# Loads, order and products of the first batch, and the place of the first chunk's forms, in a fused attention and mixture kernel

## The chip, the core and the metric

The kernel runs on one core of a Trainium2 chip. The metric is the device time of one execution in microseconds (us). Before the change, five runs gave 1661.59 to 1662.9 us, median 1661.75.

The core's engines are called by their short names in the profile: PE is TensorE (matrix products), PEld its weight loads, DVE is VectorE, ACT is ScalarE, POOL is GpSimd, SP is SyncE, which here only issues transfers (DMAs).

## The reference

All data is float32. First an attention without softmax: for each of 8 batches and 8 heads, with 576 tokens and 64 columns,

```python
kv = np.einsum('bhsd,bhse->bhde', k, v)
out = np.einsum('bhsd,bhde->bhse', q, kv)
rms = np.sqrt(np.mean(out * out, axis=-1, keepdims=True) + 1e-06)
x = out / rms * g_norm          # then (batch, token, head * column): 4608 x 512
```

Then a mixture of four experts, w1 of 512 x 1024 and w2 of 1024 x 512 each:

```python
p = domain_probs / (domain_probs.sum(-1, keepdims=True) + 1e-09)
for e in range(4):
    h = np.maximum(x @ w1[e], 0.0)
    out += p[:, e:e + 1] * (h @ w2[e])
```

## The kernel before, in words

**Chunks and steps.** The 4608 tokens are nine chunks of 512. Chunk c below 8 holds 512 tokens of batch c; chunk 8 holds the 64 tokens that are left of each batch. A step s is one chunk with one expert: s = 9 e + c, 36 steps. `up` makes h of a step, `down` or `down_deep` the second product and the sum into the output, one step later.

**Products.** A product of blocks is done by a scheme with seven products instead of eight, nested twice in most steps. It needs sums and differences ("forms") of blocks of x, w1, w2 and h, which VectorE or GpSimd computes (`combine`, line 433). `x_forms` (line 1124) makes those of a chunk's x in expert 0: four of 512 columns, seven of 256 and fourteen of 128 (25 sums), and stores them with x itself in DRAM by nine DMAs; `x_again` (line 1178) loads them for the experts 1 to 3 into five buffers `xf`. Chunk 0 in expert 0 is the exception: `up_plain` (line 1320) multiplies it in the plain way, 64 products with 512 columns (two records of the trace each), so that work can begin before any form is there. The forms of chunk 0 are made after that and serve the later experts only. Nearly all products are issued by `halves_of` (line 406): two halves of 64 output rows each; their line in the profile is 410.

**The opening** (line 688) is the attention of batch 0, by pairs of heads hp = 0 to 3. For each pair:
- `load_pair` (line 702) issues three DMAs: q with four tokens to a partition (token 4p + r, 512 tokens, 128 partitions, two pieces of 1024 bytes in each), k and v with six tokens to a partition (96 partitions, two pieces of 1536 bytes).
- `turn` (line 748) transposes q: eight products with the identity, 128 rows, 64 output rows, 128 columns (line 753).
- `key_values` (line 767): twelve products of 96 rows and 64 columns (line 772). ScalarE copies both results out of PSUM (lines 762, 785).
- `attend` (line 792): sixteen products of 64 rows and 64 columns (line 799) that use all four quarters of the array, the two row halves into two different banks `raw`.
- `scaled` (line 646): ScalarE squares (661), VectorE sums (668), ScalarE takes a root (628), VectorE inverts and scales (635 to 640, 678).
- `turn_x` (line 814): four transposes (line 817); ScalarE copies x with the gain to `xh` (line 825).

The 64 tokens that are left of batch 0 have their own load of q, four transposes (line 843) and eight products (line 861). `up_plain` needs a whole half of x (two pairs) for each of its products' operands.

**What sets the order.** Every operation is handed to a planner (`Plan`) with a key, a cost for each engine that can do it, and what it reads and writes. `layout` (line 91) plays the costs through and writes one fixed order per engine. PE takes the first operation by key that is ready, the others the one that is due first. CROSS (line 52) is the time that it counts between engines, `bus` the state of the transfers, SPARE, REACH and due times keep buffers back. Sums between SBUF buffers carry `port=True`: the planner lets VectorE and GpSimd do them one at a time, and a GpSimd sum waits for the VectorE sum planned before it (line 1734). When PE has nothing ready early on, the planner puts in fills (`idle`, line 1713: two transposes of the identity; line 1715). SP issues DMAs in planned order on eight semaphore lanes.

**Transfers in the opening.** SP issues the q, k, v of four pairs, with the gains after the second pair, then the four quarters of w1 (512 KB each, pieces of 2048 bytes), then q, k, v of batch 1, w2, and from 38.00 us the probabilities (`norm_probs`, line 446: seven DMAs, mostly pieces of 16 bytes). `result` (line 1366) writes the output rows; chunk 0's rows follow q's order of tokens, 4p + r.

Of the kernel before, what the change touches and what calls it, by code (L numbers as in the profile page):

```python
# [11 lines left out]
ALU = mybir.AluOpType  # L12
# [27 lines left out]
class Plan:  # L40
# [11 lines left out]
    CROSS, SAME, LANES = 0.3, 0.06, 8  # L52
# [38 lines left out]
    def layout(self, slots, later, idle, idle_banks, idle_until):  # L91
# [58 lines left out]
        bus, port = 3.8, 0.0  # L150
# [33 lines left out]
        while left:  # L184
# [4 lines left out]
            for eng in todo:  # L189
# [32 lines left out]
                if best is not None:  # L222
                    op = best
                    op.start, op.eng = t, eng
                    if eng == "SP":
                        busy[eng] = t + op.cost[eng]
                        bus = max(bus, t + 1.5) + op.kb / 215.0
                        op.end = bus + 0.5
                        lanes = lanes[1:] + [op.end]
                    else:  # L230
                        op.end = busy[eng] = t + op.cost[eng]
                        if op.kb:
                            op.end += 9.0 if op.kb == 512 else 8.0
# [62 lines left out]
def kernel(  # L296
# [76 lines left out]
    for kind, n in BANKS.items():  # L373
# [15 lines left out]
    slots["w2y"] = [w2y_home[:, i, :] for i in range(2)]  # L389
    later = [  # L390
        (("kv", "kvbd"), "w2y", [kv_home[:, i, :] for i in range(3)]),
# [37 lines left out]
    def combine(key, cost, out_, a, b, op, reads, writes):  # L429

        plan.add(
            key, cost,
            lambda eng: adder(eng).tensor_tensor(out=out_(), in0=a(), in1=b(), op=op),  # L433
            reads=reads, writes=writes, port=True,
        )
# [10 lines left out]
    def norm_probs(key):  # L446
        by_batch = moe_domain_probs.rearrange("(b s) e -> s b e", s=S)

        def load_all(eng):
            nc.sync.dma_start(  # L450
                out=p_all[:, 0:NR, :],
                in_=moe_domain_probs[0:NT, :].rearrange("(p r) e -> p r e", r=NR),
            )
            for r in range(NR):
                nc.sync.dma_start(
                    out=p_all[:, NR + r:B * NR:NR, :], in_=by_batch[r * P:(r + 1) * P, 1:, :])
            for bb in range(2):
                nc.sync.dma_start(
                    out=p_all[bb * REM:(bb + 1) * REM, B * NR:NBLK, :],
                    in_=by_batch[NT:S, bb::2, :],  # L460
                )
# [10 lines left out]
        plan.add(key, {"SP": 4.0}, load_all, writes=[probs], kb=72)  # L472
# [34 lines left out]
    def weights_1(e, key, step, need):  # L507
# [4 lines left out]
        for i, (n, dh, uh) in enumerate(((1, 0, 0), (2, 1, 0), (21, 0, 1), (4, 1, 1))):  # L512
# [3 lines left out]
                key + i * step, f[n],  # L516
                lambda n=n: f[n].ap[:].rearrange("p (k u) -> p k u", k=2),
                w1_src(e, dh, uh), 512 if e else 312, also=[corner[n]],
            )

        def form(k_, o, a, b, op):
# [3 lines left out]
                [f[a], f[b], corner[a], corner[b]], [f[o], corner[o]],  # L525
# [41 lines left out]
    def weights_2(e, key, step, deep):  # L567

        f = {n: Buf("big", f"w2_{e}_{n}") for n in (1, 12, 2, 3, 5, 6, 7, 4)}
        for i, (n, uh, dh) in enumerate(((1, 0, 0), (2, 1, 0), (12, 0, 1), (3, 1, 1))):  # L570
# [3 lines left out]
                w2_src(e, uh, dh), 512,  # L574
# [71 lines left out]
    def scaled(key, name, raw, n, x, blocks):  # L646
# [8 lines left out]
        def src(r):  # L655
            return raw[r].ap[0:n, 0:width].rearrange("p (b d) -> p b d", d=D)

        for r in range(2):
# [3 lines left out]
                    out=x.ap[0:n, r * width:(r + 1) * width], in_=raw[r].ap[0:n, 0:width],  # L662
                    func=ACT.Square),
                reads=[raw[r]], parts=[x],
# [10 lines left out]
        for r in range(2):  # L675
            plan.add(
# [8 lines left out]
                reads=[raw[r], rt], **{"parts" if r else "writes": [x]},  # L685
            )

    def opening(key, span, rem):
# [8 lines left out]
        at = lambda j: key + span * j / (NPAIR + 1)  # L697
        qTs, kvs = {}, {}

        splits = ((96, 6, 0),)  # L700

        def load_pair(hp):
            hs = slice(2 * hp, 2 * hp + 2)
            n = f"{b}_{hp}"
            kt, vt, qt = Buf("big", f"k{n}"), Buf("big", f"v{n}"), Buf("big", f"q{n}")
            want = key - 1 + 0.1 * hp
            load(
                want, qt, lambda qt=qt: qt.ap[:, 0:NT].rearrange("p (h x) -> p h x", h=2),
                q[b, hs, 0:NT, :].rearrange("h (p r) d -> p h (r d)", r=NR), 172,
            )  # L710
            for t, src in ((kt, k), (vt, v)):
                at_ = 0
                for rows, n_, size in splits:
                    load(
                        want, t,
                        lambda t=t, at_=at_, rows=rows, n_=n_: t.ap[0:rows, at_:at_ + 2 * n_ * D]
                        .rearrange("p (h x) -> p h x", h=2),
                        src[b, hs, size:size + rows * n_].rearrange("h (p j) d -> p h (j d)", j=n_),
                        241,
                    )  # L720
                    at_ += 2 * n_ * D
            return kt, vt, qt

        def kv_rows(t):

            at_ = 0
            for rows, n_, _ in splits:
                for j in range(n_):
                    yield [
                        t.ap[0:rows, at_ + (h * n_ + j) * D:at_ + (h * n_ + j + 1) * D]  # L730
                        for h in range(2)
                    ]
                at_ += 2 * n_ * D

        groups = ((0,), (1,), (2,), (3,))
        for g, pairs in enumerate(groups):
            n = f"{b}_{g}"
            kbank = Buf("ab", f"kv{n}")
            kv = Buf("kvbd", f"kvc{n}")
            held = []  # L740
            for o, hp in enumerate(pairs):
                kvs[hp] = kv, o
                kt, vt, qt = load_pair(hp)
                held.append((kt, vt))
                bank = Buf("ab", f"qT{b}_{hp}")
                qT = qTs[hp] = Buf("big", f"qT{b}_{hp}")

                def turn(eng, bank=bank, qt=qt):
                    for r in range(NR):
                        rs = slice(r * P, (r + 1) * P)  # L750
                        for o in range(2):
                            at = (o * NR + r) * D
                            nc.tensor.matmul(  # L753
                                bank.ap[o * D:(o + 1) * D, rs], lhsT=qt.ap[:, at:at + D],
                                rhs=ident[:],
                            )

                plan.add(
                    at(hp), {"PE": 0.82}, turn, reads=[qt], writes=[bank])
                plan.add(  # L760
                    at(hp), act(NT),
                    lambda eng, bank=bank, qT=qT: nc.scalar.activation(
                        out=qT.ap[:, 0:NT], in_=bank.ap[:], func=ACT.Copy),
                    reads=[bank], writes=[qT],
                )

            def key_values(eng, bank=kbank, held=held):
                for o, (kt, vt) in enumerate(held):
                    sets = list(zip(kv_rows(kt), kv_rows(vt)))
                    for j, (ks, vs) in enumerate(sets):  # L770
                        for r in range(2):
                            nc.tensor.matmul(  # L772
                                bank.ap[r * D:(r + 1) * D, o * D:(o + 1) * D],
                                lhsT=ks[r], rhs=vs[r], start=(j == 0),
                                stop=(j == len(sets) - 1), skip_group_check=True,
                            )

            size = len(pairs)
            plan.add(
                at(pairs[-1]), {"PE": 0.73 * size + 0.2}, key_values,  # L780
                reads=[t for ts in held for t in ts], writes=[kbank],
            )
            plan.add(
                at(pairs[-1]), act(size * D),
                lambda eng, bank=kbank, to=kv, size=size: nc.scalar.activation(
                    out=to.ap[:, 0:size * D], in_=bank.ap[:, 0:size * D], func=ACT.Copy),
                reads=[kbank], writes=[kv],
            )
            kind = ("db", "u2", "u1", "db")[g]
            raw = [Buf(kind, f"raw{n}_{r}") for r in range(2)]  # L790

            def attend(eng, raw=raw, kv=kv, pairs=pairs):
                for o, hp in enumerate(pairs):
                    for i in range(NR):
                        for c in range(2):
                            for r in range(2):
                                half = slice(r * D, (r + 1) * D)
                                at = i * P + c * D
                                nc.tensor.matmul(  # L799
                                    raw[r].ap[c * D:(c + 1) * D, (o * NR + i) * D:(o * NR + i + 1) * D],  # L800
                                    lhsT=qTs[hp].ap[half, at:at + D],
                                    rhs=kv.ap[half, o * D:(o + 1) * D],
                                )

            plan.add(
                at(pairs[-1] + 0.4), {"PE": 0.5 * size + 0.2}, attend,
                reads=[qTs[hp] for hp in pairs] + [kv], writes=raw,
            )
            x = Buf("big", f"xg{n}")
            scaled(at(pairs[-1] + 0.4), n, raw, P, x, size * NR)  # L810
            for o, hp in enumerate(pairs):
# [954 lines left out]
```

## Time and profile before

| what | value |
|---|---|
| median of five runs | 1661.75 us (1661.59 to 1662.9) |
| the profiled execution's own time | 1661.64 us |
| its span, first to last instruction | 1659.5 us |
| granted PE clock, mean | 0.999 |
| PE busy in the stretches 62 to 185, 463 to 830, 830 to 1200 us | 122.95 of 123, 366.95 of 367, 370.00 of 370 |
| PE busy from 0 to 22 us, fills among it | 19.80 of 22 |
| DMA, 2 to 16 us | 247 GB/s, share 0.99 of 16 engines |
| issue of q, k, v of pair 0 and time to landing | 0.75 + 2.9, 1.25 + 3.4, 1.75 + 4.7 us |
| issue of k, v of pair 3 and time to landing | 9.20 + 7.4, 10.53 + 7.3 us |

How to read it: "busy" of PE is the time in which at least one product is under way; fills are among it. A line of a time line has start, length, engine, line of the kernel, operation, out <- in, shape and number of records, and in brackets how long the engine had been idle and what ended that. A line of the table of stretches has the stretch, its length, busy time and number of records of PE, PEld, DVE, ACT and POOL (an engine without records is left out of the heading when only some are asked for), the granted PE clock, the busy share of the 16 DMA engines and GB/s. A line of waits has engine and line, what released it, then the sum, the number and the longest of the waits.

### The profile page before, as it was taken

To read this page: it belongs to the slowest core of one execution; us is meant where nothing else is said; L and a number is where in the kernel's file an instruction comes from. 1 tells how busy PE (TensorE), PEld (TensorE's weight loads), DVE (VectorE), ACT (ScalarE), POOL (GpSimd) and SP (SyncE) were. 2 spreads that over 40 slices of the span, in tenths; PEclk is the share of its full clock that TensorE was granted. 3 is DMA by queue.
4 is the path that set the end of the run, shared out by engine and by line. 5 is a ranking of instruction groups with operands and counts; after the bars stand their busy time and mean duration, and the time that the engine had idled before them with its cause. 6 is when DMAs were issued, how large, how long until landed. Compare 5 with 4: busy or idle time off the path is not lost.

```text
span 1659.5 us, 66359 instructions
## 1 busy us (share of the span) xinstructions
PE 1650.9 (99%) x28884; PEld 1558.2 (94%) x28884; DVE 1284.2 (77%) x2153; ACT 976.4 (59%) x2420; POOL 648.4 (39%) x649
## 2 busy tenths in 40 slices
PE   9999999999999999999999999999999999999998
PEld 6688888888899999999999999999999999999996
DVE  4778777766888687888788887888888887788874
ACT  3455555554556665666666666666666666666662
POOL 3532323214344554333345445433355444433332
PEclk9999999999999999999999999999999999999999
DMA  9876765524466444444558444444577544444442
GB/s 218 190 226 184 227 182 152 161 100 180 160 175 149 114 114 121 114 116 111 140 161 194 115 117 118 103 116 117 137 185 179 129 116 117 107 113 116 117 104 52
DMA packets 208123, 234.27 MB, mean 141 GB/s; under 512 B 97368, under 2 KB 148440, under 8 KB 207832
## 3 DMA queue, kind: packets, MB, share of 16 engines
q1 hardware_dynamic: 184760, 193.32, 38.5%
q0 software_dynamic: 23072, 36.71, 14.4%
q8 instruction: 227, 3.72, 0.9%
q14 instruction: 64, 0.52, 0.1%
HBM read 155.79 MB, written 74.19 MB: 139 GB/s over the span
## 4 chain that ended last, share of the span: by engine, by line
PE 99%; DMA 0%; SPq 0%; ACT 0%; issue 0%; DVE 0%; ACTq 0%
PE u L410 48%; PE db L410 32%; PE ab L410 15%; PE ab L1004 1%; PE ab L1031 1%; PE ab L1072 1%; DMA big<-in_q_dram 0%; PE ab L1715 0%; PE db L1040 0%; SPq L439 0%; PE ab L1093 0%; PE ab L817 0%; PE ab L753 0%; PE ab L772 0%; PE u L799 0%
## 5 line engine op out<-in xcount | busy, mean ns | idle before, releaser
L433 DVE TENSOR_TENSOR big<-big,big 128x1024 f32<-128x1024 f32 (+1 forms) x518 | 503.3, 985 | 41.0 <-ACT big L1229 17.4
L410 PE MATMUL u<-xf,big 128*64 128x128 f32 x7072 | 507.8, 273 | 0.2
L410 PEld LDWEIGHTS u<-xf,big 128*64 128x64 f32 x7072 | 410.5, 137 | 5.7 <-issue 1.8
L410 PE MATMUL u<-xf,w1y 128*64 128x128 f32 x5304 | 384.0, 273 | 0.0
L410 PE MATMUL db<-big,big 128*64 128x128 f32 (+1 forms) x4320 | 360.9, 307 | 1.4 <-ACT snap L921 1.4
L1273 DVE TENSOR_TENSOR big<-u,snap 128x256 f32<-128x256 f32 x458 | 192.1, 421 | 174.9 <-PE u L410 138.0
L410 PEld LDWEIGHTS u<-xf,w1y 128*64 128x64 f32 x5304 | 308.8, 137 | 3.4 <-issue 0.3
L1265 ACT ACTIVATE snap<-u 128x256 f32<-128x256 f32 x490 | 188.0, 384 | 197.8 <-PE u L410 159.7
L410 PEld LDWEIGHTS db<-big,big 128*64 128x64 f32 x4320 | 263.8, 137 | 41.6 <-ACT snap L921 1.6
L433 POOL TENSOR_TENSOR big<-big,big 128x256 f32<-128x256 f32 (+1 forms) x166 | 197.0, 1190 | 156.7 <-DVE big L433 88.7
L1265 ACT ACTIVATE big<-u 128x256 f32<-128x256 f32 x458 | 174.9, 384 | 90.3 <-PE u L410 64.5
L433 POOL TENSOR_TENSOR big<-big 128x512 f32<-128x512 f32 (+1 forms) x79 | 94.8, 1201 | 148.5 <-DVE big L433 95.4
L1579 ACT ACTIVATE snap<-db 128x256 f32<-128x256 f32 (+1 forms) x230 | 82.4, 358 | 101.5 <-PE db L410 93.1
L1229 ACT ACTIVATE big<-big 128x1024 f32<-128x1024 f32 x131 | 137.6, 1050 | 5.5 <-DVE big L433 2.9
L433 DVE TENSOR_TENSOR big<-big 128x512 f32<-128x512 f32 (+1 forms) x128 | 111.4, 878 | 0.0
L1265 ACT ACTIVATE u<-u 128x256 f32<-128x256 f32 x245 | 91.0, 371 | 31.1 <-PE u L410 14.8
L1617 POOL TENSOR_TENSOR big<-big 128x512 f32<-128x512 f32 x28 | 35.8, 1278 | 184.4 <-DVE big L433 168.5
L1432 POOL DMA_DIRECT2D out_dram<-big x100 | 89.6, 1128 | 46.1 <-ACT big L1409 31.4
L410 PE MATMUL db<-small,big 128*64 128x128 f32 x1416 | 106.4, 273 | 0.4 <-ACT snap L1579 0.4
L1587 DVE TENSOR_TENSOR big<-ab,snap 128x256 f32<-128x256 f32 x160 | 67.2, 420 | 38.7 <-PE ab L410 25.6
L410 PE MATMUL ab<-big,big 128*64 128x128 f32 (+1 forms) x1344 | 93.6, 278 | 0.0
L410 PE MATMUL db<-kv,big 128*64 128x128 f32 x1264 | 87.4, 273 | 0.0
(193 smaller groups left out, 2345.0 us busy)
## 6 DMA issues: line engine op xcount, KB each, us to landing
xf<-x SPq DMA_DIRECT2D x108, 512.0 KB, 3.7
out_dram<-big POOLq DMA_DIRECT2D x84, 256.0 KB, 5.6
xf<-x_h SPq DMA_DIRECT2D x81, 256.0 KB, 3.2
xf<-x SPq DMA_DIRECT2D x81, 256.0 KB, 3.7
x<-xf SPq DMA_DIRECT2D x36, 512.0 KB, 4.4
big<-in_moe_w_dram SPq DMA_DIRECT2D x31, 512.0 KB, 5.3
x_h<-big SPq DMA_DIRECT2D x18, 512.0 KB, 4.1
big<-in_moe_w_dram POOLq DMA_DIRECT2D x17, 512.0 KB, 6.8
```

The lines of the kernel that those rows point to most:

```text
L410: nc.tensor.matmul(out_[cols], lhsT=lhsT[:, cols], rhs=rhs, **kw)
L433: lambda eng: adder(eng).tensor_tensor(out=out_(), in0=a(), in1=b(), op=op),
L1004: nc.tensor.matmul(bank.ap[r * D:(r + 1) * D, o * D:(o + 1) * D], lhsT=ks[r], rhs=vs[r], start=(j == 0), stop=(j == len(sets) - 1), skip_g ...
L1031: nc.tensor.matmul(raw[r].ap[c * D:(c + 1) * D, (o * NR + t) * D:(o * NR + t + 1) * D], lhsT=qt.ap[half, col:col + D], rhs=kv.ap[half, o * ...
L1072: nc.tensor.transpose(turned[o].ap[:, r * P:(r + 1) * P], qt.ap[:, o * NT + r * P:o * NT + (r + 1) * P], ident[:])
L1229: lambda eng: nc.scalar.activation(out=b.ap[:], in_=b.ap[:], func=ACT.Relu),
L1265: lambda eng: nc.scalar.activation(out=where(), in_=ps.ap[:, 0:HN], func=ACT.Copy),
L1273: lambda eng: nc.vector.tensor_tensor(out=block(whole, a, t), in0=src.ap[:, 0:HN], in1=add_.ap[:], op=ALU.add),
L1432: nc.gpsimd.dma_start(out=dst, in_=cell(i)[parts, :], accum_op=ALU.add)
L1579: lambda eng: nc.scalar.activation(out=where(), in_=group_of(ps.ap), func=ACT.Copy),
L1587: lambda eng: nc.vector.tensor_tensor(out=cell(tq, dq), in0=group_of(src.ap), in1=group_of(add_.ap), op=ALU.add,),
L1617: lambda eng: adder(eng).tensor_tensor(out=whole(to), in0=whole(a), in1=whole(b), op=ALU.add),
```

## The change

1. **Loads.** q, k and v of a pair are each one DMA of a contiguous block, token 9p + j: 64 partitions for each of the two heads, one piece of 2304 bytes per partition. All 576 tokens come with it, so the separate load and transposes for batch 0's left tokens go.
2. **Products.** The turns of q are eighteen products of 64 rows and 64 columns per pair, the key-value products another eighteen. Their two row halves (one head each) write the two partition halves of one bank; the ninth turn is put into the key-value bank beside the sum. One copy moves both. The two results of `attend` take halves of the banks `db` (new kind "raw"), so pairs follow one another in them.
3. **Pair by pair.** Each product of `up_plain` is cut in four, one for each pair, and needs only that pair's x (`x_part`). The first quarter of w1 is loaded after the second pair.
4. **Probabilities.** Nine DMAs issued by GpSimd as its first work, in place of seven by SP from 38 us.
5. **Chunk 0's forms.** Expert 0 stores only the two halves of its x. In expert 1 chunk 0 comes fifth (chunks 1, 2, 3, 4, 0, 5, ...), and `x_first` loads the blocks, makes the 25 sums there and stores the seven results. The sums of w1 in expert 0 wait for the opening's scaling (`opened`).
6. **Output rows** of chunk 0 follow 9p + j: two DMAs of 64 rows in place of one of 128.
7. **Planner and buffers.** CROSS 0.3 to 0.2, the model of the bus, the sizes of some loads; k and v of batch 1 go to `big` buffers.

Fills in the planned order are 46 instead of 62. The diff, cut to its core:

```diff
-    CROSS, SAME, LANES = 0.3, 0.06, 8
+    CROSS, SAME, LANES = 0.2, 0.06, 8
-        bus, port = 3.8, 0.0
+        bus, port = 2.6, 0.0
-                        bus = max(bus, t + 1.5) + op.kb / 215.0
-                        op.end = bus + 0.5
+                        bus = max(bus, t + 0.6) + op.kb / 215.0
+                        op.end = bus + 1.9
...
+            for h in range(2):
+                half = slice(h * D, (h + 1) * D)
+                nc.gpsimd.dma_start(out=p_all[half, 0:NR, :], in_=first[:, h:S // D - 1:2, :])
...
             for r in range(NR):
-                nc.sync.dma_start(
+                nc.gpsimd.dma_start(
                     out=p_all[:, NR + r:B * NR:NR, :], in_=by_batch[r * P:(r + 1) * P, 1:, :])
...
-        plan.add(key, {"SP": 4.0}, load_all, writes=[probs], kb=72)
+        plan.add(-2.9, {"POOL": 9.0}, load_all, writes=[probs], kb=72)
...
+            for t, src, kb in (("q", q, 230), ("k", k, 230), ("v", v, 230)):
+                loaded[t] = Buf("big", f"{t}{n}")
+                load(
+                    key - 1 + 0.1 * hp, loaded[t], lambda t=loaded[t]: t.ap[:, 0:J * D],
+                    src[b, 2 * hp:2 * hp + 2].rearrange("h (p j) d -> (h p) (j d)", j=J), kb,
+                )
...
+            def turn(out_, qt, j):
+                for r in range(2):
+                    half = slice(r * D, (r + 1) * D)
+                    nc.tensor.matmul(
+                        out_[half], lhsT=qt.ap[half, j * D:(j + 1) * D], rhs=ident[half, half])
...
+            def key_values(eng, bank=kbank, kt=kt, vt=vt, qt=qt, turn=turn):
+                turn(bank.ap[:, D:P], qt, J - 1)
+                for j in range(J):
+                    for r in range(2):
+                        half, cols = slice(r * D, (r + 1) * D), slice(j * D, (j + 1) * D)
+                        nc.tensor.matmul(
+                            bank.ap[half, 0:D], lhsT=kt.ap[half, cols], rhs=vt.ap[half, cols],
+                            start=(j == 0), stop=(j == J - 1), skip_group_check=True,
+                        )
...
+    def x_first(c, key, step):
+        views, f = {}, {m: Buf("xf", f"xf{c}_{m}") for m in OUTER}
...
+        for m, a, b in ((5, 5, 1), (6, 6, 5), (7, 3, 7), (4, 4, 6)):
+            combine(
+                key + OUTER.index(m if m != 5 else 6) * step, either(NT), base[m], base[a], base[b],
+                ALU.subtract, [f[a], f[b]], [f[m]],
+            )
...
-            for dh in range(2):
+            for hp in range(NPAIR):
+                dh, kt = divmod(hp, 2)
...
-                    key - 0.89 + 0.01 * (i ^ 2) if i < 4 and dh == 0 else key + span * i / 8,
-                    pe(2, NT), product,
+                    key - 0.89 + 0.04 * hp + 0.01 * (i ^ 2) if i < 4 else key + span * i / 8,
+                    pe(1, NT), product, reads=[w, low, x_part[hp]], holds=[xh[dh]],
...
-    x_forms(0, 0.45)
+    for dh in range(2):
+        keep(0, f"h{dh}", x_halves(0)[dh], 512, 1.35)
...
+    CHUNKS = {e: list(range(NCH)) for e in range(E)}
+    CHUNKS[1].insert(4, CHUNKS[1].pop(0))
```

## Prediction

> **What bounds the kernel now.** I read the page first: its span, the busy shares, and the chain that ended last.
>
> ```profile
> span 1659.5 us, 66359 instructions
> ...
> PE 1650.9 (99%) x28884; PEld 1558.2 (94%) x28884; DVE 1284.2 (77%) x2153; ACT 976.4 (59%) x2420; POOL 648.4 (39%) x649
> ...
> PE 99%; DMA 0%; SPq 0%; ACT 0%; issue 0%; DVE 0%; ACTq 0%
> ```
>
> TensorE (PE) is busy 99% of the span and is 99% of the chain. So time can only come from two places: PE time that does no needed work, or fewer needed products. The waits of PE say how much idle time there is:
>
> ```profile
> PE db L410 <- ACT snap L921: 1.4, 1, 1.4
> PE ab L1715 <- POOL ident masks.py:199: 1.4, 1, 1.4
> PE ab L772 <- issue: 0.7, 1, 0.7
> PE db L410 <- ACT snap L1579: 0.4, 1, 0.4
> PE ab L753 <- DMA big<-in_q_dram: 0.2, 1, 0.2
> ```
>
> 4.1 us in all; the stage table from 62 to 1640 us shows only 0.6 us of PE idle. But the fills of line 1715 (products of the identity that serve nothing) count as busy, so the time line of PE is read next (start, length, line, records; a plain product of the program is two records, a transpose one):
>
> ```profile
> 1.37 4.10 PE L1715 MATMUL ab<-ident 128*128 128x128 f32 x18 [1.37 <-POOL ident masks.py:199]
> 5.40 1.24 PE L753 MATMUL ab<-ident,big 128*64 128x128 f32 x16
> 6.58 1.31 PE L1715 MATMUL ab<-ident 128*128 128x128 f32 x10
> 7.82 0.92 PE L772 MATMUL ab<-big,big 96*64 96x64 f32 x24
> ...
> 9.54 0.69 PE L799 MATMUL db<-kv,big 64*64 64x64 f32 x32
> 10.17 0.66 PE L1715 MATMUL ab<-ident 128*128 128x128 f32 x4
> ...
> 15.87 0.22 PE L772 MATMUL ab<-big,big 96*64 96x64 f32 x1 [0.65 <-issue]
> ...
> 30.72 1.47 PE L1715 MATMUL ab<-ident 128*128 128x128 f32 x12
> 32.13 5.37 PE L410 MATMUL u<-big,big 128*64 128x512 f32 x24
> 37.33 1.34 PE L1004 MATMUL ab<-kv 120*64 120x64 f32 x40
> ...
> 40.85 0.68 PE L861 MATMUL db<-kv,big 64*64 64x64 f32 x16
> 41.46 8.80 PE L410 MATMUL u<-big,big 128*64 128x512 f32 x40
> ...
> 61.33 3.67 PE L410 MATMUL db<-big,big 128*64 128x256 f32 x32 [1.41 <-ACT snap L921]
> ```
>
> The 62 fills, the waits for q at 11.85 (0.18) and 15.87 (0.65) and the wait at 61.33 (1.41) are what a better opening can win. The opening is paced by loads: the table of stretches gives 247 GB/s at 16 engines full from 2 to 16 us (pieces of 1024 and 1536 bytes), and 346 when w1 comes in pieces of 2048:
>
> ```profile
> 2.00:16.00 14.00, 13.17 (x223) 11.44 (x223) 2.74 (x8) 4.94 (x12) 0.00 (x0) 1.00 0.99 247
> 16.00:22.00 6.00, 6.00 (x126) 4.93 (x127) 2.68 (x10) 3.93 (x11) 2.14 (x3) 1.00 1.06 346
> 43.00:44.00 1.00, 1.00 (x6) 0.29 (x4) 0.60 (x3) 0.30 (x1) 1.00 (x1) 1.00 0.46 12
> 627.00:668.00 41.00, 41.00 (x752) 40.78 (x750) 30.89 (x48) 25.16 (x64) 18.74 (x17) 1.00 0.48 118
> ```
>
> **The sum: the opening.** I compare PE's stretch from 5.40 us to the end of the first 64 records of wide products (line 410, 512 columns). Before: at 37.33 56 of them are done; the other 8 at (50.19 - 41.46)/40 = 0.218 us each take 1.75, so the end is 39.08 and the stretch 33.68 us. After, in the order of the changed program, with durations from start to start of the next block:
> - Two more fills before the first block, 0.3 (10 warm records took 1.24, 18 early ones 4.03), and 0.2 because the first block after them was slower (1.18 against 0.97): 0.5.
> - Four attend blocks (line 799) at 0.63: 2.52. Four blocks of x transposes at 0.53: 2.12.
> - The fills that are left after that: 10, 4, 6, 4 and 2 records at 1.24, 0.58, 0.81, 0.58, 0.37: 3.58. The groups of 6 and 12 at 20.98 and 30.72 are gone.
> - 64 wide records at 0.218: 13.95.
> - The new turn and key-value blocks: per pair 18 + 18 products, 72 records of 64 rows, 64 columns; 288 in all, at r ns each. They replace blocks of 128 and 96 rows.
> - A wait ahead of the first x transpose. The key-value block of pair 1 ends at about 12.4; ScalarE then copies it (0.3), loads a table (1.28), takes the root (0.3); VectorE needs 1.7 from there to the scaled x (13.56 to 15.26 before): 16.1, while PE is there at 15.3. Wait 0.8. Queued behind it on PE is everything.
> Without the new blocks that is 23.47 us. So the opening gains 33.68 - 23.47 = 10.21 minus 0.288 r.
>
> **r is the disputed price.** No row before has such a block: two row halves and two column halves in turn, on the diagonal, into one bank. Rows near it: line 799, all four quarters: 0.63/32 = 20 ns. Lines 1004 and 772, two column halves, tall weights, 64 columns: 1.26/40 and 0.75/24 = 31. Line 861, two row halves on one column half: 0.61/16 = 38. The steady products take 54.5 ns for 128 columns with two halves side by side, so 27 for 64, and twice that, 53, if nothing overlaps. I take 28 (two side by side); ends 20 and 53. Then the blocks cost 8.06 and the opening gains 2.15 us.
>
> The Trainium skill, "TensorEngine Tiling (Array Packing)", Gotcha 1: PSUM Pressure, speaks against the change: different row tiles write to different PSUM banks and can't use the same bank at once. Line 799 obeys that (its row halves go to two banks), the new blocks don't, and no row here shows what it costs; by the rule r would be the 53 of the rival below.
>
> **The sum: the rest.** The eight turns and four transposes for the 64 left tokens: line 843's block (38.59 to 38.98, 0.39) goes, its products are in the 288. The wait at 61.33 (1.41) is for ScalarE's copy of the banks of batch 1's attend (line 921), because the first down product follows that attend at once. In the new order 16 wide records and a key-value block (3.5 + 1.2 us) stand between the two, so the copy is done by then. I count it gone. Sum: -(2.15 + 0.39 + 1.41) = -3.95 us, in general -12.01 + 0.288 r.
>
> Costed at nothing, with their cover:
> - **Loads.** Pieces of 2304 bytes: bounds 247 and 346 GB/s from the rows. v of pair 3 lands last, 4.06 MB in (w1's first 0.52 now before it): before it landed at 10.5 + 7.3 = 17.8, which is 2.2 after 2 + 3.35/0.247. So 15.9 to 20.6; PE wants it at 20.2. Batch 1's k and v for the second key-value block are wanted near 43 and are issued some 10 us earlier than at 45.04. If the cover is gone: up to 3.
> - **Probabilities.** Nine DMAs of 16-byte pieces, now from GpSimd among the opening loads. Row 43 to 44: 0.46 of all engines for 12 GB/s; 72 KB cost 2.7 us of all 16 engines. With 346 GB/s the loads keep their lead over PE even so; with 247 PE waits up to 3. GpSimd's own time (up to 1.3 us per DMA, 11.7) ends before the 19.10 at which it began on w1 before. SP's issue from 38.00 to 44.9 goes; nobody waited for SP there but loads. Other end: queue 0's mean packet, 14.4% of 16 x 1659.5 us / 23072 = 166 ns, would make it 47.7 us of all engines.
> The Trainium skill, "DMA: Bandwidth & Descriptors", Issuing engines are not separate DMA queues, says the same against the move: DMAs of all issuers share 16 engines and only issue time is saved.
> - **Chunk 0's forms** (25 sums, nine stores) leave 40 to 90 us, where PE waited for none: 0. They come back in expert 1; see the second rival.
> - **Output rows 9p+j**: two DMAs of 64 rows for one of 128, for chunk 0 alone: 12 more issues of 0.85 to 0.9 us on GpSimd, 39% busy: 0.
> - **The planner's constants** reorder everything. It counts on a hand-over of 0.2 instead of 0.3 us; the tightest one I see is 0.06 (ScalarE ends 61.27, PE starts 61.33). Gain at most 0.6 (all the idle time there), loss bounded by the tightest hand-over: 0.
>
> **Forecast.** The profiled execution took 1661.64 us (span 1659.5, 2.1 around it), 0.1 below the median 1661.75, so its sum stands for the median too: 1661.64 - 3.95 = **1657.7**. Own range: r = 20 gives 1655.4; down to 1655.0 for idle time that the new order may save; r = 28 with half a microsecond of small waits gives 1658.3. Chance 58%.
>
> **Rivals.**
> 1. *Less is left* (27%): r of 31 to 41, or loads late, or the wait of 1.41 turning up elsewhere. r = 31 gives 1658.6, r = 38 1660.6, the forecast with the wait kept 1659.1, with loads 3 late 1660.7. For it: the row of 38 ns. With r = 41.7 the change does nothing. Likeliest 1659.5.
> 2. *Slower: the shared turn of VectorE and GpSimd in expert 1* (9%). Sums between buffers are planned one at a time over both engines. Chunk 0 is the fifth chunk there, and its forms fall between 586 and 668 us. In the stretch 627 to 668 such sums take 19.65 + 14.06 (line 433, VectorE and GpSimd) + 4.51 + 1.28 (line 1617) = 39.5 of 41 us. The forms add four of 512 (0.70), seven of 256 (0.42), fourteen of 128 (0.28): 9.7 us on VectorE, and 1.5 have room. If nothing gives way, PE waits for all of them: 1657.7 + 9.7 = 1667.4. It decides from 7.3 us of waits on. Against it: the first two stages of expert 1 carry 56 such sums of 256 more, and PE was busy 81.95 of 82 us; and a sum that moves from GpSimd (1.30 for 512) to VectorE frees half its turn, with 10 us of VectorE free.
> 3. *Slower: the row halves don't overlap* (6%). r = 53: 288 x 0.053 = 15.3, +3.3: 1665.0. It is slower from r = 41.7, by over 0.2% from r = 53. Tiny packets at 166 ns are in the same place: loads at half of 346, v of pair 3 at 2 + 23.5 + 2.2 = 27.7, 7 late: 1665.2.
>
> **Chances.** 0.2%, about what a measurement of this kernel can tell from no change, is 3.3 us. Faster by more: 58%. Within: 27%, rival 1. Slower by more: 15%, rivals 2 and 3. The range 1655.0 to 1662.5 takes in the forecast and rival 1 and leaves out the slow rivals and a little below.
>
> **What would show it.** Right: the turn and key-value blocks at 0.9 and 1.1 us; 46 fills; the first wide product near 21 us and the 64th record near 37; no wait of PE for a load before 37 us; none near 61; chunk 0's forms with no PE wait from 586 to 668. Wrong: records of 40 ns or more in the new blocks, q or v as releaser of PE, a PE wait for VectorE in expert 1.

## The result, and the profile after

The changed kernel takes 1666.07 us (median of 41 runs, 1664.57 to 1667.94), the kernel before in the same comparison 1662.6 us (median of 77, 1660.59 to 1667.85): a ratio of 1.0020, 95% interval 1.0015 to 1.0024. It is slower by 0.2%. The forecast was 1657.7. Executions with a mean granted PE clock of 0.998 are some 1 to 3 us longer than those with 1.0, so where most of five runs have it, as in one experiment below, the median lies well above the profiled execution.

The page of the changed kernel, the three lines that answer to those of before:

```profile
span 1664.4 us, 66539 instructions
...
PE 1651.6 (99%) x28992; PEld 1559.1 (94%) x28992; DVE 1252.9 (75%) x2146; ACT 982.0 (59%) x2415; POOL 695.5 (42%) x681
...
PE 96%; DMA 1%; DVE 1%; issue 1%; POOL 0%; ACT 0%; SPq 0%; POOLq 0%; DVEq 0%; ACTq 0%
```

The span is 4.9 us longer, PE is busy 0.7 us longer, so some 4.2 us are new idle time. The view of waits, PE's lines (engine and line, releaser, sum, number, longest):

```profile
PE ab L725 <- issue: 1.7, 1, 1.7
PE db L765 <- issue: 1.4, 1, 1.4
PE ab L1701 <- POOL ident masks.py:199: 1.4, 1, 1.4
PE db L414 <- ACT snap L1559: 0.7, 2, 0.5
PE u L414 <- DVE big L1249: 0.6, 1, 0.6
PE u L414 <- ACT small L1241: 0.5, 1, 0.5
PE u L414 <- ACT big L1241: 0.5, 1, 0.5
PE u L414 <- ACT u L1241: 0.5, 1, 0.5
```

Two things are new: two stalls put down to "issue" (the engine waited for nothing that the profile shows), and half a dozen waits of about half a microsecond for copies and a sum out of PSUM (the banks that PE writes its results to), far behind the opening. The wait of 1.41 at 61.33 is gone, as forecast. The time line of PE places the stalls (batch 0's key-values, turns and attends):

```profile
13.42 0.34 PE L765 MATMUL db<-kv,big 64*64 64x64 f32 x6
15.20 0.62 PE L765 MATMUL db<-kv,big 64*64 64x64 f32 x26 [1.44 <-issue]
...
19.14 0.74 PE L725 MATMUL ab<-ident,big 64*64 64x64 f32 x19
21.56 0.50 PE L725 MATMUL ab<-ident,big 64*64 64x64 f32 x10 [1.67 <-issue]
...
24.42 1.08 PE L414 MATMUL u<-big,big 128*64 128x512 f32 x4
...
32.68 7.95 PE L414 MATMUL u<-big,big 128*64 128x512 f32 x36
40.45 1.34 PE L940 MATMUL ab<-big,big 120*64 120x64 f32 x40
```

Both stalls lie in the middle of a block whose data were there, after 6 and after 19 of 32 records. The first wide product starts at 24.42 (before 21.78, forecast 21), the 64th wide record ends at 40.45 (before 39.08, forecast 36.9). The 39.08 is the prediction's reckoning, without the blocks of lines 1004 and 843 that stand among the last of the 64; in the trace of before they end at 40.85, and after the change no such block stands there.

Two counts carry the rest of this text. **Records before a stall:** summed along the time line, the stalls come after record 222 and after record 349 of PE, 127 apart. The 0.65 at 15.87 in the profile of before comes after record 221, so it is probably of the same kind. **Records per stretch:** from 463 us on PE is full, so what is lost shows as fewer records in a stretch of the same length. Before:

```profile
830.00:1200.00 370.00, 370.00 (x6784) 370.00 (x6782) 301.54 (x474) 231.62 (x582) 153.80 (x149) 1.00 0.51 129
1200.00:1570.00 370.00, 370.00 (x6784) 370.00 (x6782) 300.87 (x482) 232.62 (x586) 163.03 (x155) 1.00 0.54 134
```

After:

```profile
830.00:1200.00 370.00, 369.41 (x6760) 368.73 (x6758) 296.80 (x470) 231.94 (x580) 173.12 (x156) 1.00 0.52 128
1200.00:1570.00 370.00, 368.62 (x6740) 367.52 (x6738) 285.01 (x480) 234.70 (x585) 169.85 (x157) 1.00 0.54 133
```

24 and 44 records fewer at 370/6784 = 54.5 ns are 3.7 us, more than the idle time shown (0.59 + 1.38). The ends of products are modelled in this profile, so part of a wait can count as busy; that this is the whole difference is not shown.

### The profile page after: what moved, and what is told of

Its sections match the earlier page's. It is cut to its first block, busy times and chain, and to the rows that moved or that the text cites. A ratio compares the mean times of both kernels' runs of the same rounds, so it can differ in the third digit from the quotient of the medians.

```text
span 1664.4 us, 66539 instructions
## 1 busy us (share of the span) xinstructions
PE 1651.6 (99%) x28992; PEld 1559.1 (94%) x28992; DVE 1252.9 (75%) x2146; ACT 982.0 (59%) x2415; POOL 695.5 (42%) x681
## 3 DMA queue, kind: packets, MB, share of 16 engines
q8 instruction: 228, 3.74, 0.9%
## 4 chain that ended last, share of the span: by engine, by line
PE 96%; DMA 1%; DVE 1%; issue 1%; POOL 0%; ACT 0%; SPq 0%; POOLq 0%; DVEq 0%; ACTq 0%
PE u L414 46%; PE db L414 31%; PE ab L414 14%; PE ab L967 1%; PE ab L940 1%; PE ab L1008 1%; DMA big<-in_moe_w_dram 1%; PE ab L1701 0%; DVE big L437 0%; PE ab L725 0%; PE ab L745 0%; POOL big L1597 0%; DVE big L1597 0%; PE db L976 0%; DMA small<-in_q_dram 0%
## 5 line engine op out<-in xcount | busy, mean ns | idle before, releaser
L437 DVE TENSOR_TENSOR big<-big,big 128x1024 f32<-128x1024 f32 (+1 forms) x592 | 549.3, 950 | 26.6 <-ACT big L1205 8.6
L414 PE MATMUL u<-xf,big 128*64 128x128 f32 x6496 | 474.6, 273 | 0.3 <-ACT snap L1241 0.2
L414 PEld LDWEIGHTS u<-xf,big 128*64 128x64 f32 x6496 | 381.3, 137 | 5.1 <-ACT snap L1241 1.0
L437 POOL TENSOR_TENSOR big<-big,big 128x256 f32<-128x256 f32 (+1 forms) x157 | 207.0, 1323 | 195.9 <-DVE big L437 103.4
L437 POOL TENSOR_TENSOR big<-big 128x512 f32<-128x512 f32 (+1 forms) x94 | 114.4, 1221 | 146.0 <-DVE big L437 92.9
L1412 POOL DMA_DIRECT2D out_dram<-big x122 | 106.8, 1078 | 27.4 <-ACT big L1389 22.1
L414 PE MATMUL db<-small,big 128*64 128x128 f32 (+1 forms) x1528 | 116.7, 274 | 0.0
L437 DVE TENSOR_TENSOR big<-big 128x512 f32<-128x512 f32 (+1 forms) x121 | 102.0, 853 | 0.0
L1389 ACT ACTIVATE big<-big,p_all 128x256 f32<-128x256 f32 x204 | 96.0, 500 | 3.8 <-POOL big L1597 2.9
L414 PEld LDWEIGHTS db<-small,big 128*64 128x64 f32 x1528 | 90.8, 137 | 0.9 <-issue 0.2
```

The lines of the kernel that those rows point to most:

```text
L414: nc.tensor.matmul(out_[cols], lhsT=lhsT[:, cols], rhs=rhs, **kw)
L1389: lambda eng: nc.scalar.activation(out=cell(i, half), in_=ap(), func=ACT.Copy, scale=prob()),
L1412: nc.gpsimd.dma_start(out=dst, in_=cell(i)[parts, :], accum_op=ALU.add)
```

## The experiments

Theory **P**: the small waits come from the one constant of the planner, the hand-over CROSS, that I had costed at nothing. Rival **M**: from the moved forms, buffers or transfer model. Theory **I**: the stalls are PE waiting for its own instructions. Rivals **Q** (the probabilities' small packets) and **H** (a hazard of the two-half blocks).

### CROSS, undone in the changed kernel and done alone in the kernel before

```diff
-    CROSS, SAME, LANES = 0.2, 0.06, 8
+    CROSS, SAME, LANES = 0.3, 0.06, 8
```

> The changed kernel with one constant of the planner as before: hand-overs between engines counted with 0.3 us in place of 0.2. Theory P (the small waits of TensorE come from an order planned for hand-overs that are too tight): TensorE's idle time from 62 to 1640 us falls from 4.0 us to below 1.5, and the time by some 2.5 to 3.5 us, to about the time of the kernel before (ratio 1.000). Rival M (they come from the moved forms of chunk 0, the other buffers of batch 1 or the cost model of the DMAs): the idle time stays above 3 us and the ratio at 1.002. The two stalls of 1.4 to 1.7 us in the opening stay by both.

Measured: 1662.22 us against 1662.29 before, ratio 0.9999 (0.9991 to 1.0008). The opening's stalls stayed: 1.11 us after record 222, 1.55 us after record 349. The records of the two stretches are back:

```profile
830.00:1200.00 370.00, 370.00 (x6784) 370.00 (x6782) 305.61 (x476) 232.00 (x583) 157.81 (x152) 1.00 0.51 128
1200.00:1570.00 370.00, 370.00 (x6784) 370.00 (x6780) 304.23 (x482) 232.56 (x587) 164.95 (x158) 1.00 0.53 134
```

PE's idle time from 62 to 1640 us fell from 4.02 to 1.97, not below 1.5: 1.4 us between 62 and 185 are left (0.8 for VectorE at line 1396, 0.5 for ScalarE). From the end of the 64th wide record to the end of the span the changed kernel takes 1623.95 us, this one 1619.43: 4.5 us for one constant. In sum the profiled span is 0.4 us above that of before (1659.9 against 1659.5).

> The kernel before with hand-overs counted with 0.2 us in place of 0.3, and nothing else. Theory P: TensorE's idle time from 62 to 1640 us rises from 0.6 us to 3 or more, the time by 2.5 to 3.5 us (ratio 1.0015 to 1.002). Rival M: the idle time stays below 1.2 us and the ratio within 1.0005 of 1.

The opposite edit. Measured: 1663.41 us, ratio 1.0007 (0.9998 to 1.0016): by the time alone unclear, and well below the 2.5 us that P asked for. The profile speaks for P: span 1662.2 against 1659.5, idle time from 62 to 1640 us 3.4 us against 0.6, and in the stretches:

```profile
830.00:1200.00 370.00, 369.42 (x6762) 368.74 (x6760) 279.36 (x471) 233.28 (x581) 166.41 (x150) 1.00 0.51 128
1200.00:1570.00 370.00, 369.41 (x6762) 368.73 (x6759) 283.24 (x479) 233.46 (x586) 172.21 (x156) 1.00 0.53 132
```

22 records short in each, in a kernel with none of the other parts. All profiles of this text fall into the same two groups: the nine kernels planned with 0.3, however else they differ, have 6780 to 6784 records in each of the two stretches, the five planned with 0.2 have 6730 to 6762. So it is not one unlucky order. What the waits look like, in the changed kernel: PE,

```profile
906.01 0.61 PE L414 MATMUL u<-xf,big 128*64 128x128 f32 x8
907.16 1.09 PE L414 MATMUL u<-xf,w1y 128*64 128x128 f32 x16 [0.54 <-ACT small L1241]
```

(a wait of 0.53 or 0.54 us for the same copy stands between 906 and 908 us in all five kernels with 0.2), and ScalarE:

```profile
906.72 0.38 ACT L1241 ACTIVATE small<-u 128x256 f32<-128x256 f32 x1 [1.42 <-PE u L414]
```

The products end at 906.62, the copy runs from 906.72 to 907.10, and the next products into the same bank start at 907.16. The hand-overs themselves are 0.10 and 0.06 us by these modelled ends, shorter than 0.2. So 0.2 is not too short for one hand-over. The order that comes out of it here uses a bank again at once with nothing between; in these stretches the profiles of 0.3 show no such wait. Why the planner's choices fall out so was not traced further.

### The probabilities back on SP, the forms back in expert 0

The nine DMAs are issued by `nc.sync` in place of `nc.gpsimd`, and:

```diff
-        plan.add(-2.9, {"POOL": 9.0}, load_all, writes=[probs], kb=72)
+        plan.add(key, {"SP": 5.0}, load_all, writes=[probs], kb=72)
```

> The changed kernel with the nine transfers of the probabilities back on the SP queue at the place in the order that the kernel before gives them (about 40 us), rows still 9p+j. Theory Q (the 16-byte packets slow the opening's loads, and with them whatever TensorE stalls for at 13.8 and 19.9 us): the two stalls of 1.44 and 1.67 us fall below 0.7 each, the first wide product comes near 22.5 us and the time falls by 1.5 to 2.5 us. Rival I (TensorE waits there for its own instructions, at a fixed count of records, 222 and 349): the stalls stay at the same records with over 1 us each, and the time is within 0.7 us of the changed kernel, but for other small waits in the body.

Measured: 1667.2 us, ratio 1.0032 (1.0020 to 1.0045). The stalls come after the same records 222 and 349, with 0.67 and 2.08 us, in sum 2.75 against 3.11; the 64th wide record ends at 40.60. Neither forecast is met whole: the first stall is below the 0.7 of Q and not above the 1 us of I, and the time is 1.1 us above the changed kernel instead of within 0.7. But no packet of 16 bytes is near, the two stops stay at their counts, and nothing is won: the packets are not what makes PE stop there.

```diff
-    for dh in range(2):
-        keep(0, f"h{dh}", x_halves(0)[dh], 512, 1.35)
+    x_forms(0, 0.45)
...
-    CHUNKS[1].insert(4, CHUNKS[1].pop(0))
```

> The changed kernel with chunk 0's forms made in expert 0 as before and the chunks of expert 1 in their natural order. If the moved forms make the small waits of the body (rival M): idle time of TensorE from 62 to 1640 us falls from 4.0 us to below 1.5 and the time by about 3 us. By theory P: the idle time stays above 2.5 us in all, spread over the whole body, and the time is within 1 us of the changed kernel. If the room that the move made at 40 to 90 us was needed, waits of 1 us or more appear there.

Measured: 1668.91 us, ratio 1.0035 (1.0023 to 1.0048). The median of the five is 2.8 us above the changed kernel, more than P allowed; the profiled execution (1666.04, span 1664.3 against 1664.4) is not. Nothing is won, and the stretches from 830 us on have 6761 and 6736 records, about those of the changed kernel. PE waits 0.97 us at 81.53 for a load of v, which the changed kernel does not; the expectation had named 1 us there. So the forms are not the cause, and the other parts of M (buffers, transfer model) are spoken against by the two experiments on CROSS alone. The same edit with CROSS at 0.3:

> The kernel of the first experiment with chunk 0's forms made in expert 0 as before and the chunks of expert 1 in natural order, so that the move of the forms is the only difference. If the move is worth nothing (as the prediction said): the time is within 0.7 us of the first experiment's (ratio to before 0.9995 to 1.0004) and TensorE's idle time from 463 to 830 us stays below 0.3 us in both. If the forms cost their place in expert 0: waits of 0.7 us or more more than in the first experiment between 40 and 185 us.

Measured: 1662.56 us, ratio 0.9997 (0.9988 to 1.0006), idle time from 463 to 830 us 0.16 in both; the profiled span is 0.7 us above that of the first experiment (1660.6 against 1659.9), the median 0.3. The move of the forms is worth nothing that these runs can tell.

### The stalls: how long the refill takes

Every profile of a kernel with the new blocks so far stalls after records 222 and 349, whatever stands there: after the second count the turn of pair 3 in three of them (CROSS 0.2), the attend of pair 2 in the others (CROSS 0.3). That speaks against H as well. The page's table of queues counts one packet of instructions per 127 records (28992/228; 3.74 MB/228 = 16.4 KB each); that this queue is PE's own is inferred from the count:

```profile
q8 instruction: 228, 3.74, 0.9%
```

> Beside the kernel of the first experiment (hand-over 0.3), in which TensorE stalls 1.11 us at record 222 and 1.55 us at record 349: the loads of w1's quarters 2 to 4 are now issued only once the turn of pair 2 has run (about 16 us in place of 10 to 13), so that the queues are shorter when the second refill of instructions is on its way. Theory I (TensorE waits for the next 16 KB of its own instructions, 127 records, which travel behind the loads that are queued): the first stall stays at record 222 with 0.9 to 1.5 us, the second, at 349, falls below 0.7 us. Rival H (the stalls belong to the two-half blocks themselves, a hazard in one bank or a late semaphore): both stay within 0.3 us. If the quarters are now late, TensorE waits for a load before 35 us.

Measured: 1662.6 us, ratio 1.0 (0.9992 to 1.0009), stalls 1.24 and 1.47 us. It tried nothing: only the planner knew of the wait, and SP issued the quarters from 10.85 us as ever. With a wait that holds:

```diff
+            if e == 0 and i == 1:
+                gate.append(plan.add(
+                    -1.2, act(1),
+                    lambda eng, n=n: nc.scalar.activation(
+                        out=f[n].ap[0:1, 0:1], in_=turned[2].ap[0:1, 0:1], func=ACT.Copy),
+                    reads=[turned[2]], writes=[f[n]],
+                ))
```

> The late quarters of w1 again, now with a wait that the hardware keeps: one ScalarE copy of a single element of pair 2's turned q into quarter 2 of w1 (overwritten by the load), so that quarters 2 to 4 are issued from about 16 us on. In the first try they were issued at 10.9 to 14.9 us, as without the edit, so it tried nothing. Beside the kernel with hand-over 0.3 (stalls of 1.11 us at record 222 and 1.55 at record 349). Theory I with queued loads (the 16 KB of instructions wait behind the loads): the stall at 349 falls below 0.7 us, the one at 222 to 0.5 to 1.1. Theory I with a fixed time (from the passing of one boundary to the delivery of the next but one takes 6.4 us whatever is queued): both stay within 0.3 us. A wait for a quarter of w1 before 35 us may take the place of what is won.

Measured: the quarters are issued from 16.91 us. Time line of PE in this kernel:

```profile
13.18 0.33 PE L774 MATMUL db<-kv,big 64*64 64x64 f32 x4
14.40 0.62 PE L774 MATMUL db<-kv,big 64*64 64x64 f32 x27 [0.90 <-issue]
...
18.87 0.69 PE L774 MATMUL db<-kv,big 64*64 64x64 f32 x32
19.39 1.11 PE L734 MATMUL ab<-ident,big 64*64 64x64 f32 x32
...
21.08 1.08 PE L414 MATMUL u<-big,big 128*64 128x512 f32 x4
...
32.36 6.23 PE L414 MATMUL u<-big,big 128*64 128x512 f32 x28
38.42 1.34 PE L949 MATMUL ab<-big,big 120*64 120x64 f32 x40
```

Record 349 is in the middle of the block at 18.87, and there is no stall at all. Without the hold the same place reads:

```profile
19.14 0.46 PE L765 MATMUL db<-kv,big 64*64 64x64 f32 x15
21.15 0.47 PE L765 MATMUL db<-kv,big 64*64 64x64 f32 x17 [1.55 <-issue]
```

The packet of instructions is seen between 16 and 17 us with the hold, between 18 and 19 without it. So the refill waits behind loads that are queued, and a fixed time falls.

The starts and lengths of these packets in the traces tie them to the stalls. Without the hold the packet begins 3.86 us after PE goes on behind record 222 (14.68 to 18.54), with it 1.70 us (14.40 to 16.10). In all 17 stalls by "issue" at these counts, the 0.65 of the kernel before at 15.87 among them, PE goes on 1.3 to 1.9 us after such a packet has ended; in the changed kernel the packets end at 13.36 and 20.16, the stalls at 15.20 and 21.56. Where a packet had ended some 1.7 us or more before PE came to the record, there is no such stall.

The 64th wide record ends 2.05 us earlier, at 38.42. The time is 1661.41 us, ratio 0.9992 (0.9983 to 1.0001): most of it is given back, because what SP issues behind the held DMA is late too (the next weights from 40.71 us in place of 39.04). VectorE stands idle for 6.29 us until 51.20 for a load of weights, and PE waits 0.95 us at 59.85 and 1.60 us at 68.09 for what VectorE does after that. Part of this has another cause: one VectorE operation of 128 x 16 at 56.71 took 2.28 us, where the same took 0.17 without the hold (see the last section).

### Fewer records: whole turns

```diff
-                for j in range(J - 1):
-                    turn(bank.ap[:, j * D:(j + 1) * D], qt, j)
+                for i in range(NR):
+                    cols = slice(i * P, (i + 1) * P)
+                    nc.tensor.transpose(bank.ap[:, cols], qt.ap[:, cols], ident[:])
...
+                    lambda eng, bank=kbank, r=r, to=other: nc.vector.tensor_copy(
+                        out=to.ap[(1 - r) * D:(2 - r) * D, 0:D],
+                        in_=bank.ap[r * D:(r + 1) * D, 0:D]),
...
-                            half = slice(r * D, (r + 1) * D)
-                            at = i * P + c * D
+                            half = slice(c * D, (c + 1) * D)
+                            at = i * P + r * D
+                            held = (kv if c == r else other).ap[half, 0:D]
```

> Beside the kernel of the first experiment: batch 0's q is turned by four transposes of 128 x 128 per pair (4 records) in place of 32 products of 64 x 64 (32 records); the two heads then lie side by side in columns, and each pair's key-values are copied crosswise into the other half by two VectorE copies. So 112 records less ahead of the wide products, about 325 to the first one in place of 437, and only the boundary at 222 lies before it. Theory I: the first stall is still at record 222, now inside the key-value block of pair 2, with 0.3 to 1.2 us; the one at 349 lies past the first wide product, with 0 to 1.2 us; the first wide product comes by 21.5 us, the 64th record ends near 38.5, the time is 1 to 2.5 us below the kernel before (ratio 0.9985 to 0.9994). Rival H (the record count is not what limits): stalls follow the blocks of two halves wherever they are, the 64th record ends within 0.5 us of 40.5, and the ratio stays within 0.0004 of 1.

Measured: 1660.54 us, ratio 0.9985 (0.9976 to 0.9994). No stall by "issue" is left:

```profile
14.31 0.66 PE L731 MATMUL ab<-ident,big 128*128 128x128 f32 x4 [1.02 <-DMA big<-in_q_dram]
...
17.16 1.22 PE L746 MATMUL ab<-big,big 64*64 64x64 f32 x36
...
22.12 1.08 PE L414 MATMUL u<-big,big 128*64 128x512 f32 x4
...
31.42 7.95 PE L414 MATMUL u<-big,big 128*64 128x512 f32 x36
39.20 1.34 PE L951 MATMUL ab<-big,big 120*64 120x64 f32 x40
```

Records 222 and 349 are passed at about 17.5 and 24 us, after the refills (packets that end at 14.65 and 22.00). The wait is now for pair 2's q, which is 1.02 us late. I had expected 0.3 us or more of stall after record 222, a first wide product by 21.5 and the 64th record near 38.5: direction right, sizes off.

> The two edits of the experiments on late quarters of w1 and on whole turns together, hand-over 0.3. By theory I: one stall of 0.3 to 1.2 us at record 222, under 0.5 us at 349, the first wide product by 21 us and the time 1.5 to 3 us below the kernel before (ratio 0.998 to 0.999). By rival H: as the whole turns alone.

Since the hold of its expectation held nothing (as in the first try), this is the whole turns once more in a slightly different order: 1660.78 us, ratio 0.9988 (0.9979 to 0.9997), no stall, no wait for q either, the 64th record at 38.76.

> Whole turns with hand-over 0.3, and the probabilities back on the SP queue near 40 us. With whole turns alone TensorE waited 1.02 us for pair 2's q at 14.31, the first wide product came at 22.12 and the 64th record ended at 39.20. If the 16-byte packets slow the opening's loads: the wait for q falls below 0.5 us, the 64th record ends by 38.6, the time is 0.3 to 1 us below that of whole turns alone (ratio to before 0.998 to 0.9985). If they do not: all within 0.3 us. Nine issues on the SP queue near 40 us may delay batch 1's or w2's loads: then a wait of TensorE for a load after 40 us.

Measured: 1659.88 us, ratio 0.9985 (0.9976 to 0.9994), the lowest of all and below both kernels. The wait for q is gone, the 64th record ends at 38.63, and since PE is earlier again, the stall after record 222 is back in small:

```profile
15.94 0.51 PE L746 MATMUL ab<-big,big 64*64 64x64 f32 x10
16.79 1.02 PE L746 MATMUL ab<-big,big 64*64 64x64 f32 x26 [0.34 <-issue]
```

By the ratio it is not apart from the whole turns alone. That the packets were what delayed q is not shown: in the run before this one they come as early, and q is not late there. The price that the expectation named did come: PE waits 0.85 us at 80.68 for a load of v.

> Whole turns, hand-over 0.3, probabilities on the SP queue near 40 us, and quarters 2 to 4 of w1 held until pair 2's q is turned. If the queue in front of q, k and v is what TensorE waits for at 14 us, that wait is gone and the 64th record ends near 38; if the quarters are now late, a wait for them appears between 24 and 35 us and the time is above that of the whole turns alone (1660.5).

Measured: 1663.16 us, ratio 1.0003 (0.9994 to 1.0011). The 64th record ends at 38.24 and no wait for a quarter of w1 appears, but VectorE is idle for 9.50 us until 53.30 for weights issued later, and PE then waits 2.49 us at 57.15. In this profile the granted clock is also 0.50 from about 57 to 63.7 us, right behind that wait, where one block of line 987 takes 2.58 us instead of 1.16. The hold costs more than it wins, but the 1663.16 is not the price of late weights alone.

> The changed kernel itself on the chip of this call. By theories P and I: stalls at records 222 and 349 of 1 to 1.8 us, 2.5 to 4 us of idle time of TensorE from 62 to 1640 us, ratio to before 1.0015 to 1.003.

Measured: 1665.91 us, ratio 1.0023 (1.0014 to 1.0032), stalls 0.88 and 1.69 us after records 222 and 349, and 6762 and 6740 records in the two stretches. The profiled execution is 1667.84: the granted clock is 0.50 in it from about 22.6 to 26 us, and the 64th wide record ends at 41.45.

## Why the prediction was wrong

Against its own sum the profiled span is 8.85 us too long (1664.4 against 1659.5 - 3.95). Of that 3.52 are in the opening (end of the 64th wide record 40.45 against 36.93) and 5.33 behind it.

1. **The step that failed most: "The planner's constants reorder everything ... Gain at most 0.6 ..., loss bounded by the tightest hand-over: 0."** Undoing this constant alone takes 4.5 us off the profiled span behind the opening and brings the ratio from 1.0020 to 0.9999. The tightest hand-over bounds one hand-over, not what another order of 28992 records does. I had named the reordering and then priced it as if it were a wait. With PE full and 0.6 us of idle time there, a reorder had little to win and much to lose. Why the order for 0.2 is the worse one stays open.
2. **A term that was missing: the refill of instructions.** 1.44 + 1.67 = 3.11 us. The row was shown, "0.65 <-issue" at 15.87, and read as a wait for q, which the weight load behind it did wait for; the packet of instructions that ended at 14.16, 1.71 us earlier, puts it with the stalls. The change doubles the records of a turn (16 to 36 per pair, the ninth included) and makes those of a key-value block 36 instead of 24, so PE reaches the next boundary before the 16 KB for it have come through a full queue.
3. **r was a little too low.** The 288 new records took about 9.1 us, start to start and without the stalls, or 32 ns each, with 28 taken: some 1.0 us more (0.2 of it I had put down apart). That is the lower end of rival 1 (31 to 41). The row halves do overlap in one bank, so rival 3 is out. The Trainium skill, "TensorEngine Tiling (Array Packing)", Gotcha 1: PSUM Pressure, says that different row tiles can't use one bank at once, by which I had estimated 53; this measurement differs from it. (Twice 27.25 is 54.5 and not 53, which would have made rival 3 1665.3; nothing else hangs on it.)
4. **The wait of 0.8 for the first x did not come**, presumably because the stall before it gave VectorE the time. Attends, fills and wide products together took some 0.3 to 0.4 more than their rows.
5. **The wait at 61.33 (1.41) is gone and line 843's block too**, but with CROSS at 0.3 only 0.99 of the 1.80 us is seen behind the opening: 1.4 us of waits between 62 and 185 us have come in place of it. That was in rival 1 ("turning up elsewhere").
6. **Rival 2 did not happen.** From 586 to 668 us PE is busy 82.00 of 82 us, and all 25 sums of chunk 0's forms are there, 16 on VectorE and 9 on GpSimd between 627 and 668.
7. **Loads and probabilities** at nothing: right for the order of arrival (no wait of PE for a load in the opening of the changed kernel). In one of the whole-turn kernels, where PE is earlier, q was 1.02 us late.

None of the rivals gave the slower time; parts of rival 1 happened (r, and waits elsewhere for the one at 61.33), and the 9% and 6% for a slower kernel stood on other causes. The 3.5 us by which the median is slower (1666.07 against 1662.6) go away with that one constant undone. The rest of the change came to nothing in the median: in the spans 1.0 us was won behind the opening and 1.4 lost in it.

The Trainium skill, "Runtime: NRT & Kernel Launch", Instruction fetch mechanics, says that instructions are refilled in blocks of 16 KiB, 256 each, and that crossing a boundary costs "one DMA tail-bump, mostly hidden". The blocks agree with the runs: 16.4 KB per packet, and 127 records with a product and a weight load each. The cost does not, where records are short and the queues full: 0.34 to 2.08 us in the stalls above.

## What to carry to other kernels

A constant of a scheduler is an edit of the whole program: build the change with it and without it, and compare records per stretch of equal length, which shows small losses that idle time hides. Where an engine that is fed with many short instructions stalls for "issue", count its records from the start; a fixed count means its own instructions, and then fewer and larger instructions, or a shorter DMA queue at that moment, help. A wait that holds back one transfer holds back all that its queue issues behind it.

## What the runs showed of the hardware that was not expected

- PE stops after records 222 and 349 in all seven profiles with the new turn and key-value blocks and loads that nothing holds back, 127 records and one packet of 16.4 KB apart. There the second stop ends 6.4 to 6.8 us after the first. With three loads held back until 16.91 us the same refill is there in under 5 us (record 222 passed at 14.40, record 349 at 19.11 without a stop).
- Two row halves of 64 x 64 products in turn, on the diagonal, into one bank: about 32 ns per record on average, nearly as fast as two column halves (31).
- Hand-overs of 0.10 us (PE to ScalarE) and 0.06 us (ScalarE to PE) around a copy of 0.38 us, by the modelled ends of the products.
- Normalising the probabilities, one VectorE operation of 128 x 144, took 2.00 us at about 33 us after the change and 0.37 us before it. GpSimd was in a sum of 128 x 1024 then, which ended 0.17 us earlier. The 2.28 us at 56.71 in the kernel with the held quarters ended 0.03 us behind such a sum, and an operation of 1.68 us at 64.13 there 0.03 us behind the next one. So small VectorE operations can last until a GpSimd sum is done; not all beside one do, and why is not shown.
- The granted PE clock fell to 0.50 for 6.8 us behind a PE wait of 2.49 us (the last kernel with the hold) and for 3.4 us some 1.5 us behind a stall of 1.69 us (the changed kernel run again). It stayed at 1.00 behind stalls of 1.67 and 2.08 us in other profiles, so the wait alone does not settle it.
